# Gate loop and low-rank mixer on one core: a newly planned order of 2,210 operations

## The chip, the cores and the metric

The kernel runs on one core of a Trainium2 chip. Its time is the device time of that core in microseconds (us); three runs of the kernel before are given, and the profile describes one further execution. The engines are TensorE (PE in the profile, its weight loads PEld), VectorE (DVE), ScalarE (ACT), GpSimd (POOL) and SyncE (SP). Each works through its own queue in order.

## What is computed

Two blocks, one behind the other. The first is a recurrence over 768 steps with complex gates for 4 x 8 heads of width 48; the second mixes over the sequence through a matrix of rank 32 and then over channels:

```python
mag = np.sqrt(a_re * a_re + a_im * a_im)
scale = np.minimum(mag, 0.999) / (mag + 1e-06)      # a_re, a_im are multiplied by it
for t in range(S):                                   # S = 768
    S_re, S_im = ar*S_re - ai*S_im + k[t] v[t]^T,  ar*S_im + ai*S_re
    y[t] = q[t] @ S_re
x = y, as (batch 4, 768, 384)
h = x.transpose(0, 2, 1) @ U @ V                     # U 768 x 32, V 32 x 768
u = x + h.transpose(0, 2, 1)
out = u + np.maximum(u @ w_ch1, 0.0) @ w_ch2         # 384 -> 1536 -> 384
```

U, V, w_ch1 and w_ch2 arrive as 64-bit floats, which the kernel turns into 32-bit ones itself.

## The kernel before

**Tiling.** The sequence is cut into chunks of 128 steps: 6 for each batch element, 24 in all (`NCH`, `NT`). Two chunks make a group (`GC`, 12 groups).

- `gates(g)` works on a group: squares, logarithms and exponentials of the gates (`magnitudes`), sums along the chunk as products with a triangular matrix (PE tiles `es ps` and `ph`, lines 690 to 762), their exponentials `es`, angles `F` and waves `cs` (`turns`, `waves`). From group 3 on the operands are split into two parts first (`GS`, lines 677, 678, 750, 751). For each chunk but the first of a batch element POOL adds the last row of the angles before it to the new ones by a small DMA (line 742, `gate<-F`).
- `prep(i)` weighs q and k of a chunk by `es` and `cs` on DVE (`qk`, `QKC`), transposes them on PE in 64-row tiles (`tr`, line 817) and copies them out on ACT (`QK`).
- `chain(i)` does the chunk's own products (`inner`, `dk`, `y`: lines 846, 866, 895, 903), all in 64-row or 64-column tiles, and leaves the chunk's output in `xo`.
- `mixer(m)` works on two chunks: the rank-32 products (`rank`, `mixed`), transposed input `uTp`, the first channel matrix (`up`, line 992, or a scheme with fewer products, `few`, line 1104) and the second (`down`, lines 1193 and 1236). For the first two chunks the first channel product runs ahead of the rank-32 step and is then corrected by four small products (`up more`, line 1032, tiled by 32 rows); DVE adds each correction (line 1038) and so frees the PSUM bank for the next. There are two banks for `up` and `down` tiles, six for the rest.
- `single` and `weights` turn the weights (lines 583 to 589), and three differences of parts of w_ch2 are formed (line 617, `stage`, ops 88 to 90).
- `judge` (lines 1362 to 1379) checks that the fast way is valid: DVE collects extremes (`least`, line 712; `bad`, line 658), a product counts the violations (op 2208, `bad ps`), and DVE writes the count into `flag` (op 2209, line 1378; op 2207 makes its last operand). At the end every engine loads `flag` (line 1396) and branches on it (line 1406) around a general version of the kernel, which isn't run here.

**The order.** Nothing is issued when it is written down. `PE(...)`, `ACT(...)`, `DVE(...)`, `POOL(...)` and `SP(...)` each add an operation to a `Plan`, with a cost, a rank, what it reads and writes, and, for PE, `way`: a code of the tiling that its products use (0 the whole array, 1 64 columns, 3 64 x 64, 4 32 rows, 5 64 rows). Operations are numbered as they are added, 0 to 2209; "op 692" is such a number. `Plan.order` then issues them in the sequence of the constant `ORDER`, after asserting that each comes behind what it needs and that ring buffers are free. As every engine's queue is in order, `ORDER` fixes the five queues; across queues semaphores decide. An operation is several instructions (16 transpositions for a `tr`, 6 for a `down`, 8 for a `few`).

`SPARE` names operations of PE ahead of which idle products are issued: `idle(n)` (lines 1379 to 1388) multiplies the identity matrix into a PSUM tile that the following operation overwrites, two PE instructions each. Nobody reads them.

Some numbers that come up later: op 0 loads the triangular matrix `prefix_z`, op 3 is its copy on POOL, op 4 its scaling on ACT; op 95 is the first table load of ACT, ops 91 to 94 the loads of the first gates, op 96 their squares; op 199 is the first `tr`; ops 655 and 658 are the `es ps` products of group 4 (chunks 8 and 9), op 648 an ACT step ahead of them, op 683 the last wave that op 691 needs; op 691 is the DVE product that makes the first operand `QKC` of chunk 6, op 692 its transposition; ops 416, 419, 422 and 425 are the corrections, ops 417, 418, 420, 421, 423, 424, 426 and 427 DVE's adds behind them; ops 1750 and 1752 are the angle of one late chunk and the cast of the next chunk's angles, with op 1751, POOL's small transfer, between them.

Of the kernel before, what the change touches and what calls it, by code (L numbers as in the profile page):

```python
# [15 lines left out]
OP = mybir.AluOpType  # L16
# [99 lines left out]
)  # L116

SPARE = {
    125: 2, 135: 9, 184: 1, 199: 21, 203: 1, 223: 2, 250: 3, 412: 2,
}  # L120

DUMP = None
# [195 lines left out]
def kernel(  # L318
# [154 lines left out]
    w2 = singles.tile([128, KF, DM], FP, name="w2")  # L473
# [19 lines left out]
    def w2_of(x, y):  # L493

        return w2.rearrange("p (j x) m -> p j x m", x=2)[:, :, x, y * DH:(y + 1) * DH]
# [960 lines left out]
```

## Time and profile before

| | us |
|---|---|
| three runs | 559.97, 560.68, 565.65 |
| median | 560.68 |
| span of the profiled execution (first to last instruction) | 559.4 |
| first product of PE starts | 11.05 |
| last addition of DVE starts | 554.54 |
| busy in the span: PE, DVE, ACT, POOL | 533.3, 432.3, 317.7, 32.2 |

The profiled execution's own time is known as its span, 559.4 us; the time around it isn't shown apart. The fastest run lies 0.6 us above this span and the median 1.3.

How to read the lines: a group has the source line, engine, operation, output and inputs with their shapes and a count, then the busy time, the mean in ns of one, and the idle time ahead of it with what ended most of it. A wait has the engine and line that waited, whom it waited for, the total, how often and the longest. In the timeline and in the chain the first number is the start and the second the length. A row of the windows has the stretch, its length, and the busy time of PE, weight loads, DVE, ACT and POOL with the number of instructions, then the clock granted to TensorE (1.00 is full), the share of DMA time and GB/s. "q" behind an engine means its sequencer. For a transfer the last number is the median time from issue to landing.

### The profile page before, as it was taken

How to read it: one execution, taken by the hardware profiler on the slowest of the kernel's cores; microseconds unless marked ns; L12 is line 12 of the kernel's file. 1: busy time of each engine (PE TensorE's matmuls, PEld its weight loads, DVE VectorE, ACT ScalarE, POOL GpSimd, SP SyncE). 2: the span in 40 equal slices, each digit the busy share in tenths (PEclk: the TensorE clock that was granted, in tenths of full speed). 3: DMA queues.
4: the chain of work that ended last, by engine and by line, in shares of the span. 5: the costliest groups of instructions: out<-in, count | busy, mean ns of one | idle time of the engine just before them, and what ended most of it. 6: DMA issues, size and time to landing. Idle time of an engine off the chain costs nothing.

```text
span 559.4 us, 16683 instructions
## 1 busy us (share of the span) xinstructions
PE 533.3 (95%) x7242; PEld 481.8 (86%) x7242; DVE 432.3 (77%) x828; ACT 317.7 (57%) x553; POOL 32.2 (6%) x61
## 2 busy tenths in 40 slices
PE   2899999989999999999999999999999999999996
PEld 1677786867799997999999997899999989999996
DVE  6999989899799998898896976977572726728352
ACT  6889999894657869576567855861323322111110
POOL 1000000000011000101001001001000000000000
PEclk9999999989999999999999999999999999999999
DMA  9969876331333254133342235020011000000001
GB/s 222 198 145 201 195 182 184 91 52 37 85 66 80 45 107 76 37 69 65 60 91 51 57 52 110 16 40 27 9 36 36 4 2 22 8 8 22 21 9 33
DMA packets 150687, 39.90 MB, mean 71 GB/s; under 512 B 145912, under 2 KB 147408, under 8 KB 150608
## 3 DMA queue, kind: packets, MB, share of 16 engines
q1 hardware_dynamic: 148400, 34.43, 31.2%
q0 software_dynamic: 2208, 4.35, 2.3%
q8 instruction: 58, 0.95, 0.7%
q14 instruction: 21, 0.17, 0.1%
HBM read 33.60 MB, written 4.76 MB: 69 GB/s over the span
## 4 chain that ended last, share of the span: by engine, by line
PE 53%; DVE 20%; issue 7%; ACT 4%; DMA 3%; POOL 0%; SPq 0%; DVEq 0%; ACTq 0%; POOLq 0%
PE down L1236 20%; PE few L1104 17%; PE dk L866 3%; PE tr L817 3%; ACT gate L439 2%; DMA gate<-F 2%; PE inner L846 2%; DVE xo L445 2%; PE y L903 2%; DVE QKC L442 2%; PE up L992 1%; DVE qk L442 1%; PE y L895 1%; DVE GS L751 1%; DVE GL L671 1%
## 5 line engine op out<-in xcount | busy, mean ns | idle before, releaser
L1112 ACT COPY h<-few 128x512 f32<-128x512 f32 x60 | 34.8, 584 | 86.0 <-PE few L1104 84.6
L439 ACT ACTIVATE gate<-gate 128x768 f32<-128x768 f32 (+2 forms) x74 | 65.9, 901 | 16.6 <-DVE GS L751 9.0
L1236 PE MATMUL down<-w,h 128*128 128x192 f32 x396 | 72.7, 330 | 0.2 <-DVE xo L445 0.2
L1236 PEld LDWEIGHTS down<-w,h 128*128 128x128 f32 x396 | 64.5, 190 | 2.7 <-DVE xo L445 1.1
L445 DVE TENSOR_TENSOR xo<-down,xo 128x192 f32<-128x192 f32 (+1 forms) x79 | 29.8, 386 | 41.9 <-PE down L1236 39.7
L823 ACT COPY QK<-tr 112x512 f32<-112x512 f32 x96 | 50.0, 596 | 20.3 <-PE tr L817 20.1
L1104 PE MATMUL few<-extra,w 128*128 128x128 f32 x400 | 50.2, 276 | 0.1
L1104 PEld LDWEIGHTS few<-extra,w 128*128 128x128 f32 x400 | 47.6, 192 | 0.7 <-PE mixed L961 0.4
L1116 DVE CUSTOM_DVE_ANT_1 h<-few,h 128x512 f32<-128x512 f32 x60 | 40.2, 686 | 8.1 <-PE few L1104 4.3
L442 DVE TENSOR_TENSOR QKC<-qk,cs 128x768 f32<-128x768 f32 x48 | 44.5, 952 | 0.8 <-PE tr L817 0.6
L445 DVE TENSOR_TENSOR h<-few,h 128x512 f32<-128x512 f32 x30 | 20.5, 687 | 23.8 <-PE few L1104 12.6
L1236 PE MATMUL down<-stage 128*128 128x192 f32 x198 | 38.0, 329 | 0.5 <-DVE xo L445 0.5
L1180 POOL DMA_DIRECT2D out_dram<-xo x32 | 18.1, 573 | 276.8 <-DVE xo L445 248.5
L1236 PEld LDWEIGHTS down<-stage 128*128 128x128 f32 x198 | 32.6, 190 | 1.7 <-DVE xo L445 1.4
L992 PE MATMUL up<-uT,w 128*128 128x256 f32 x144 | 32.4, 382 | 0.2 <-ACT uT L981 0.2
L1104 PE MATMUL few<-gate,w 128*128 128x128 f32 x240 | 31.8, 277 | 0.1
L817 PEld LDWEIGHTS tr<-ident,QKC 64*112 64x112 f32 x768 | 25.2, 135 | 7.5 <-DVE QKC L442 2.5
L436 ACT ACT_TABLE_LOAD x24 | 30.8, 1283 | 1.1 <-PEq L1440 0.7
L817 PE MATMUL tr<-ident,QKC 64*112 64x64 f32 x768 | 29.8, 226 | 1.4 <-DVE QKC L442 1.4
L992 PEld LDWEIGHTS up<-uT,w 128*128 128x128 f32 x144 | 27.0, 190 | 4.4 <-ACT uT L981 0.6
L1104 PEld LDWEIGHTS few<-gate,w 128*128 128x128 f32 x240 | 29.1, 192 | 0.3 <-PE few L1104 0.2
L439 ACT ACTIVATE cs<-F 128x384 f32<-128x384 f32 x48 | 24.1, 520 | 8.1 <-DVE F L765 7.9
(161 smaller groups left out, 1106.2 us busy)
## 6 DMA issues: line engine op xcount, KB each, us to landing
stage<-in_moe_w_ch_dram SPq DMA_DIRECT2D x12, 768.0 KB, 5.4
gate<-in_a_im_dram SPq DMA_DIRECT2D x24, 192.0 KB, 3.0
gate<-in_a_re_dram SPq DMA_DIRECT2D x24, 192.0 KB, 3.7
qk<-in_q_dram SPq DMA_DIRECT2D x24, 192.0 KB, 4.4
qk<-in_k_dram SPq DMA_DIRECT2D x24, 192.0 KB, 3.6
VP<-in_v_dram SPq DMA_DIRECT2D x24, 192.0 KB, 3.9
out_dram<-xo POOLq DMA_DIRECT2D x12, 192.0 KB, 2.2
out_dram<-xo POOLq DMA_DIRECT2D x20, 96.0 KB, 1.9
```

The source lines that it names most:

```text
L436: ACT(1.37, rank, lambda: nc.scalar.preload_act_table_set(name), writes=[TABLE])
L439: return nc.scalar.activation(out=o, in_=i, func=f, **kw)
L442: nc.vector.tensor_tensor(out=o, in0=a, in1=b, op=OP.mult)
L445: nc.vector.tensor_tensor(out=o, in0=a, in1=b, op=OP.add)
L817: nc.tensor.transpose(out=get(*ps[r])[0:DQ, h], in_=get(*qkc)[at, h].rearrange("p u d -> p (u d)")[:, 0:DQ], identity=ident[at, at], tile_ ...
L823: nc.scalar.copy(out=get(*QK)[:, u].rearrange("p (h t) -> p h t", t=CH)[:, :, r * HC:(r + 1) * HC], in_=get(*ps[r])[0:DQ])
L992: nc.tensor.matmul(out=get(*ps)[:, e], lhsT=w1[:, f, (ff + e) * 128:(ff + e + 1) * 128], rhs=get(*uT)[:, f], start=(f == 0), stop=(f == KD ...
L1104: nc.tensor.matmul(out=get(*ps)[:, q], lhsT=w()[:, q * 128:(q + 1) * 128], rhs=v[0](), start=(n == 0 and q == 0), stop=True, skip_group_ch ...
L1112: ACT(c_act(n3 * CH) - 0.045, RU, lambda i=i, k=k: nc.scalar.copy(out=at(i, k), in_=get(*ps)), [ps], [o])
L1116: DVE(c_dve(n3 * CH), RU, lambda i=i, k=k: nc.vector._custom_dve(dve_ops.TENSOR_ADD_SAT, out=at(i, k), in0=get(*ps), in1=at(i, k), s0=math ...
L1180: queue.dma_start(out=out[b, c * CH:(c + 1) * CH, lo:hi], in_=get("xo", i)[:, lo:hi])
L1236: nc.tensor.matmul(out=get(*to)[:, part], lhsT=x(j), rhs=y[:, j], start=(first and j == 0), stop=(j == KH - 1), skip_group_check=not first)
```

## The change

`ORDER` is replaced whole: the same 2,210 operations, with the same numbers, in another sequence. `SPARE` is replaced: 36 idle products ahead of five operations in place of 41 ahead of eight. And one dependency is written down that was implicit in the old sequence: the product with the part of w_ch2 that DVE turns in place for the second pair of chunks (line 1306) now names that step, `("turned w2", 0)`. No operation is added or removed. The new order is said to be planned from traced durations, counting each change of TensorE's tiling.

The diff, cut to the lines of `ORDER` that matter here (95 lines in the file; each side's first, then around ops 655 to 692, then around op 1751, then the flag and the end):

```diff
 ORDER = (
-    95, 93, 91, 94, 0, 92, 150, 5, 11, 96, 99, 149, 100, 152, 97, 3, 151, 4, 98, 101, 194, 115, 112, 2, 116, 102, 195, 113, 106, 104, 196, 117, 114,
...
-    85, 652, 651, 653, 86, 655, 654, 465, 658, 656, 425, 87, 738, 657, 659, 661, 426, 660, 88, 662, 666, 739, 427, 89, 422, 682, 683, 685, 691, 686,
-    664, 667, 695, 692, 663, 668, 423, 701, 789, 715, 702, 693, 788, 669, 696, 694, 424, 703, 716, 740, 719, 416, 704, 814, 698, 90, 726, 813, 697,
...
-    1749, 1447, 1890, 1750, 1775, 1789, 1450, 1867, 1751, 1858, 1866, 1448, 1776, 1471, 1451, 1470, 1449, 1474, 1777, 1473, 1472, 1778, 1752, 1475,
...
-    1886, 1671, 1662, 1663, 1667, 1664, 1669, 1668, 1672, 1673, 1670, 1903, 1674, 1904, 2208, 1905, 1677, 2209, 1906, 1907, 1675, 1678, 1925, 1676,
...
-    2203,
+    0, 3, 4, 95, 91, 93, 92, 96, 99, 97, 98, 94, 101, 100, 102, 5, 103, 104, 115, 112, 106, 105, 113, 114, 7, 151, 107, 6, 117, 118, 120, 119, 121,
...
+    649, 456, 465, 83, 650, 651, 652, 460, 653, 84, 85, 132, 457, 616, 461, 654, 86, 655, 618, 656, 87, 658, 659, 657, 660, 81, 666, 458, 459, 661,
+    428, 738, 619, 681, 88, 683, 682, 425, 429, 504, 667, 426, 427, 691, 422, 505, 739, 692, 695, 668, 684, 430, 693, 696, 669, 694, 423, 685, 789,
...
+    1499, 1496, 1501, 1497, 1500, 1890, 1814, 1484, 1751, 1505, 1752, 1502, 1507, 1753, 1498, 1506, 1817, 1776, 1818, 1508, 1800, 1509, 1511, 1513,
...
+    2192, 2188, 2184, 2199, 2186, 2193, 2189, 2187, 2191, 2194, 2190, 2207, 2195, 2196, 2197, 2198, 2047, 2120, 2200, 2201, 2202, 2203, 2121, 2208,
+    2209, 2125,
 )
 
 SPARE = {
-    125: 2, 135: 9, 184: 1, 199: 21, 203: 1, 223: 2, 250: 3, 412: 2,
+    125: 3, 135: 5, 199: 23, 227: 4, 412: 1,
 }
...
-            product(one, 0, lambda j: of(0, 1)[:, j], w2_of(0, 1), names, first=False)
+            product(one, 0, lambda j: of(0, 1)[:, j], w2_of(0, 1), lambda half: names(half) + [("turned w2", 0)], first=False)
...
-                                                                    op=OP.subtract), [("w2s", 0)], ALL_W2)
+                                                                    op=OP.subtract), [("w2s", 0)], ALL_W2 + [("turned w2", 0)])
```

158 rows, old and new, of the table ORDER are left out of this document.

## The prediction

> **What bounds the kernel now.** First the page: busy times, then the slices.
>
> ```profile
> span 559.4 us, 16683 instructions
> PE 533.3 (95%) x7242; PEld 481.8 (86%) x7242; DVE 432.3 (77%) x828; ACT 317.7 (57%) x553; POOL 32.2 (6%) x61
> ...
> PE   2899999989999999999999999999999999999996
> ...
> DVE  6999989899799998898896976977572726728352
> ```
>
> TensorE (PE) is busy for 95% of the span, and the order leaves its 7242 products as they are. So a new order can only take from the other 26 us, from the changes of tiling, and from products that run slowly. In the first eight slices or so (to about 120 us) DVE is nearly always busy; after that PE alone is full. The second view is the waits, here of the first 131 us; its last row is from the waits after that.
>
> ```profile
> PE es ps L696 <- DVE GL L445: 11.1, 1, 11.1
> DVE GL L671 <- ACT GL L439: 3.6, 1, 3.6
> ...
> DVE GS L750 <- DMA gate<-F: 5.3, 5, 3.5
> ```
>
> PE starts at 11 us. DVE waits once 3.6 us for ACT, and later 3.5 us for one small transfer. The third view is the windows, the fourth the timeline around 120 us, where PE waits for DVE in a knot: at the corrections (L1032) and at the transpositions of chunk 6 (L817).
>
> ```profile
> 117.10:120.50 3.40, 1.51 (x8) 0.71 (x10) 3.40 (x6) 3.37 (x7) 0.00 (x0) 1.00 0.46 88
> 120.50:127.30 6.80, 6.60 (x120) 5.36 (x119) 6.80 (x9) 5.73 (x10) 0.77 (x1) 0.50 0.51 76
> ...
> 118.25 0.42 DVE L1038 CUSTOM_DVE_ANT_0 extra<-up,extra 128x256 f32<-128x256 f32 x1
> 118.58 1.35 DVE L617 TENSOR_TENSOR stage<-w 128x1152 f32<-128x1152 f32 x1
> 118.72 0.29 PEld L1032 LDWEIGHTS up<-V,more 32*128 32x128 f32 x2 [1.38 <-DVE extra L1038]
> ...
> 122.45 0.90 PEld L817 LDWEIGHTS tr<-ident,QKC 64*112 64x112 f32 x16 [0.92 <-DVE QKC L442]
> ```
>
> The columns after the window's length are busy PE, weight loads, DVE, ACT, POOL, then the granted clock. From 117.1 PE works 1.51 of 3.4 us; a DVE instruction of 1.35 us (L617) stands between two of those (L1038) that free its banks. In the 6.8 us after that the clock is 0.50.
>
> **The change, term by term.** The sum is made against the profiled execution, 559.4 us. That lies 1.3 under the median of the runs, 560.68, which I add at the end.
>
> *Changes of tiling.* On PE's queue, idle products included, the planner's tiling code changes 166 times in the old order and 153 times in the new (counted from ORDER). The price is read from the chain:
>
> ```profile
> 450.56 2.15 PE down L1236 x12
> ...
> 495.15 1.95 PE down L1236 x12
> ...
> 20.53 4.85 PE L1388 MATMUL tr<-ident 128*128 128x128 f32 x42
> ```
>
> Twelve "down" products that follow full-array products and precede others take 1.95 us; between tiled products (L866 before, L895 behind) they take 2.15. Two changes cost 0.20 us, one 0.10. Thirteen fewer: 13 x 0.10 = **-1.3** (0 if all of them lay in waits). The idle products go from 41 to 36. I cost them at nothing: they stand before products whose operands DVE has not made yet, as op 199. Without that cover five would be worth 5 x 0.23 = 1.2 us (the last row: 21 of them, two matmuls each, in 4.85 us).
>
> *The head.* The new order puts the ACT copy of prefix_z (op 4) and the transfer behind it (op 0) ahead of the first table load and the gate loads.
>
> ```profile
> 0.74 1.28 ACT L436 ACT_TABLE_LOAD   x1 [0.74 <-PEq L1440]
> ...
> 2.75 0.71 SPq L531 DMA_DIRECT2D prefix_z<-in_spans_dram  x1
> ...
> 4.97 0.84 ACT L439 ACTIVATE gate<-gate 128x768 f32<-128x768 f32 x1 [2.95 <-DMA gate<-in_a_re_dram]
> ...
> 6.18 0.65 POOL L535 CAST prefix_r<-prefix_z 128x128 fp32r<-128x128 f32 x1 [3.94 <-DMA prefix_z<-in_spans_dram]
> 6.87 0.31 ACT L439 ACTIVATE prefix_z<-prefix_z 128x128 f32<-128x128 f32 x1 [1.06 <-POOL prefix_r L535]
> ...
> 7.67 0.84 ACT L439 ACTIVATE gate<-gate 128x768 f32<-128x768 f32 x1
> ...
> 9.38 0.52 ACT L439 ACTIVATE GL<-GL 128x384 f32<-128x384 f32 x1
> ```
>
> The transfer took 3.4 us from issue to the cast. Issued at 0.7 it lands at about 4.1; cast 0.65, copy 0.31 and table load 1.28 put the squares at 6.3 at most, not 4.97: up to +1.4. Queued behind the waiting copy is every ACT instruction, and DVE and PE wait for them. Against it, the two ACT instructions of chunk 1 in the last rows (0.84 and 0.52) no longer stand between the steps of chunk 0's chain: -1.4. I take the head at **0**, between -1.4 and +1.4; from there to the first transposition DVE's queue is the bound. On SP the small TD writes move ahead of the loads of `qk` of chunk 1, so SP stands until ACT has made `es` of chunk 1, and these loads stand behind it. DVE needs them only after chunk 0's two operands are made; that covers them, and if it didn't, DVE's wait would be the price. On POOL output stores change places, which nobody waits for.
>
> *DVE ahead of chunk 6.* Of the 168 operations in DVE's queue ahead of op 691, the last one before chunk 6's first transposition (op 692), six move behind it and none comes in: one L617, one `mixed` add, one `uT` copy, three `least`.
>
> ```profile
> L617 DVE TENSOR_TENSOR stage<-w,stage 128x1152 f32<-128x1152 f32 x2 | 2.7, 1350 | 0.0
> L445 DVE TENSOR_TENSOR xo<-mixed,xo 128x384 f32<-128x384 f32 x24 | 12.3, 550 | 0.5 <-PE mixed L961 0.5
> L983 DVE COPY uT<-uTp 128x384 f32<-128x384 f32 x12 | 6.5, 552 | 0.4 <-PE uTp L977 0.2
> L712 DVE TENSOR_TENSOR least<-least,T 112x16 f32<-112x16 f32 x12 | 2.0, 168 | 0.1
> ```
>
> 1.35 + 0.55 + 0.55 + 3 x 0.17 = 2.96 us; an instruction starts 0.09 before the end of the one ahead (118.25 + 0.42 against 118.58), so 2.96 - 6 x 0.09 = 2.4. Of PE's own products ahead of op 692 one `uTp` operation moves behind it (three products like the idle ones, 3 x 0.115 = 0.3) and has to be made up later; the rest are the same. PE's waits so shrink by 2.4 - 0.3: **-2.1**. Ends: -3.0, and 0 if ACT, not DVE, sets op 691.
>
> *The half clock.* Op 692 no longer waits right behind the corrections, and no L617 stands between ops 426, 427 and 423, 424, so I expect no stretch like 117.1 to 120.5 and no half clock. Its price, from the chain:
>
> ```profile
> 125.44 1.89 PE tr L817 x32
> ...
> 443.96 1.04 PE tr L817 x32
> ```
>
> The same 32 transpositions take 1.89 us in it and 1.04 at full clock. Of the 4.85 us from 122.45 to 127.30 that is 4.85 x (1 - 1.04 / 1.89) = 2.2 lost; some products there are not set by the clock. **-2.0** (0 to -2.2). [...] The windows show the fall right behind a stretch that was thin, not idle, so I go by them.
>
> *The late knot.*
>
> ```profile
> 341.85 0.55 DVE L765 SCALAR_TENSOR_TENSOR F<-F,ph 128x384 f32<-128x384 f32 x1 [1.12 <-ACT F L439]
> ...
> 347.40 0.36 DVE L750 CAST GS<-gate 128x384 fp32r<-128x384 f32 x1 [3.48 <-DMA gate<-F]
> ...
> 350.29 0.92 PE L961 MATMUL mixed<-r,V 64*128 64x192 f32 x8 [1.60 <-DVE G L442]
> ```
>
> Between F (op 1750, ready at 342.40) and the cast that needs the transfer from it (op 1752) DVE has two operations, and the transfer takes until 347.40; DVE stands, and `mixed` waits 1.60. In the new order eleven DVE operations stand between the two. **-1.6** (0 if another of the fifteen such transfers takes its place).
>
> *The end.* Ops 2207 to 2209 form the flag that chooses the general path. In the old order it is there at 438; in the new one its product (op 2208) is PE's last and its cast (op 2209) DVE's last. Every engine loads the flag and branches on it before it can finish.
>
> ```profile
> L1378 DVE CAST flag<-bad ps x1: 138/138/138, 438.1 to 438.1; 1x1 int32<-1x1 f32 x1
> ...
> 542.51 0.54 POOL L1180 DMA_DIRECT2D out_dram<-xo  x1 [15.08 <-DVE xo L445]
> ...
> out_dram<-xo POOLq DMA_DIRECT2D x20, 96.0 KB, 1.9
> ...
> L1396 POOLq TENSOR_LOAD <-flag x1: 493/493/493, 542.5 to 542.5; - x1
> ...
> L1406 PEldq COMPARE_BRANCH x2: 90/1912/3735, 552.0 to 554.7; - x2
> ...
> L1451 POOLq EVENT_SEMAPHORE x4: 17/17/17, 558.6 to 559.3; - x4
> L1451 POOLq DRAIN x3: 46/112/3974, 548.3 to 559.1; - x3
> ...
> 554.54 0.36 DVE L445 TENSOR_TENSOR xo<-down,xo 128x192 f32<-128x192 f32 x1 [0.42 <-PE down L1236]
> ```
>
> POOL needs 9.8 us from its load of the flag (542.5) to the end of its drain (548.3 + 4.0); some 1.1 of it it waits for its last store (issued at 542.5, landed 1.9 later, while its load and branch of the flag take 0.8), which will be long done; so 8.7. Today that is hidden behind PE. In the new order the flag is ready behind the last add, at about 555.0 on the old time; POOL then drains until 563.7, and its closing semaphores (558.6 to the end, 0.8) put the end at 564.5: **+5.1**. Ends: if the drain takes 0.11, its median, the end is 560.6, +1.2; PE's own branch of 3.7 us gives +1.0; if the landing still counts, +6.2.
>
> Sum: 559.4 - 1.3 - 2.1 - 2.0 - 1.6 + 5.1 = 557.5; with 1.3 for the median, **558.8**.
>
> **The rivals.** *A short end.* POOL's other two drains take 0.05 and 0.11 us, so the long one may be a wait for something that is over by then; against it, it starts at 548.3 with its stores landed. Time: 558.8 - 3.9 = 554.9.
> *The front gives nothing, and it ends slower.* ACT is nearly as full as DVE up to 120 us, and its queue ahead of the wave that op 691 needs (op 683) is only three operations shorter. If the copy of prefix_z costs ACT its 1.4 us at the head, op 692 starts no earlier: 558.8 + 2.1 + 2.0 = 562.9. It decides if chunk 6's first transposition starts at 122 us or later. For it: the 3.6 us for which DVE waited for ACT. Against it: that very ACT step (op 648) has five operations less in front.
> *A new thin stretch.* The new order has less PE work ahead of the `es` products of group 4 (op 655: an `up`, a `mixed` and two `uTp` operations fewer), so PE can now wait there for DVE. If a window gets thin, the clock halves for another 6.8 us: up to half of it lost, 3.4, on top of the front's loss 562.9 + 3.4 = 566.3.
> *The tiling count does nothing*, since the drains lie in waits: 558.8 + 1.3 = 560.1.
>
> **How the numbers follow.** Forecast as summed, with the tiling count or without: 0.50. Short end 0.27; front lost 0.13; thin stretch 0.10. The likeliest case has its own range of 556 to 561. With every end at its best (-1.4, -1.3, -3.0, -2.2, -1.6, +1.0) it is 552.2, at its worst (+1.4, 0, 0, 0, 0, +6.2) 568.3. For 8 in 10 I take 553 to 565: the short end and the lost front are in it, the thin stretch and the corners are not. One per cent, about what a measurement of this kernel can tell from no change, is 5.6 us: faster means under 555.1, slower over 566.3. Faster: most of the short end (0.20) and a corner of the forecast (0.06), 0.26. Slower: half of the thin stretch and a late wait not seen (0.12). Within: 0.62.
>
> **What would show it.** Changes: twelve "down" products in a row keep 1.95 and 2.15. Chunk 6: its first transposition at about 120, not 122.45, and a granted clock of 1.00 from 113 to 131. Late knot: the wait of L750 for `gate<-F` under 2 us in sum. End: the last add at about 547.5 (554.5 less 7.0), the `flag` cast behind it, then POOL's load, branch and a drain of 4 us, and some 10 us between the last add's start and the end, not 4.9. The prediction is wrong if the drain is short, if PE's waits in the first 131 us are not smaller, or if a new wait of over 2 us stands on PE behind 131.

## The result, and the profile after

The changed kernel takes 566.0 us (median of 8 runs, 564.57 to 567.45); the kernel before took 561.6 beside it. The ratio is 1.0076, with a 95% interval of 1.0052 to 1.0101: slower by three quarters of a per cent. The forecast was 558.8, with a range of 553 to 565. Two single runs stand far off, one of the kernel before here (2982.67 us) and one of more_changes below (1068.71); the ratios leave them out. The profiled execution of the changed kernel took 566.48 us, with a span of 564.7 (559.4 before).

The page of the changed kernel, its first lines and PE's row of the slices:

```profile
span 564.7 us, 16665 instructions
PE 529.3 (94%) x7232; PEld 479.7 (85%) x7232; DVE 435.8 (77%) x828; ACT 321.9 (57%) x554; POOL 32.3 (6%) x61
...
PE   2889999999999999999999999999999999999992
```

PE is busy for 4.0 us less (533.3 before), since ten idle matmuls and thirteen changes of tiling are gone and, as shown below, 3.4 us less pass at half clock; and yet the span is 5.3 us longer. The last slice of PE reads 2 where it read 6: something stands behind PE's last product. The views of three source lines at the end, and the timeline there:

```profile
L1396 POOLq TENSOR_LOAD <-flag x1: 493/493/493, 554.9 to 554.9; - x1
...
L1406 POOLq COMPARE_BRANCH  x2: 38/39/40, 555.5 to 557.2; - x2
...
L1451 POOLq EVENT_SEMAPHORE  x4: 17/17/17, 563.9 to 564.6; - x4
...
L1451 POOLq DRAIN  x3: 46/112/3973, 559.9 to 564.4; - x3
```

```profile
554.49 0.36 DVE L445 TENSOR_TENSOR xo<-down,xo 128x192 f32<-128x192 f32 x1 [1.39 <-PE down L1236]
554.76 0.14 DVE L1378 CAST flag<-bad ps 1x1 int32<-1x1 f32 x1
```

The flag is there at 554.90, POOL loads it at once, branches until 557.2, and its drain of 3.97 us starts at 559.9 and ends at 563.9; the closing semaphores take the rest. From the start of the last add to the end are 10.2 us, where there were 4.9. So the end went as forecast (+5.3 for +5.1). But the last add starts at 554.49, where it started at 554.54; the forecast was 547.5. **Of what the front and the late knot were to give, nothing is left at the end.**

Where it went shows best as a lag. For each operation I added up the usual duration of PE's real products ahead of it (for each kind of operation, the lower quartile in both traces of the time from its start to the next one's, and 0.10 more at a change of tiling; the idle ones left out), and took that from its start in the trace. What is left is time in which PE stood, ran slowly or did idle products. The difference of the lags, after less before:

| at | before: start, work ahead, lag | after | difference of the lags |
|---|---|---|---|
| first product | 11.05, 0, 11.05 | 9.92, 0, 9.92 | -1.1 |
| op 692, chunk 6's first transposition | 122.45, 87.9, 34.5 | 121.51, 88.0, 33.5 | -1.0 |
| op 431, first of the `down` products | 131.07, 94.4, 36.6 | 130.57, 95.6, 35.0 | -1.7 |
| op 1968, the last `rank` | 456.89, 413.8, 43.1 | 458.99, 414.5, 44.5 | +1.4 |
| op 2201, the last `down` | 553.37, 509.5, 43.9 | 553.31, 508.2, 45.1 | +1.2 |

The forecast was -2.1 at op 692, -4.1 at op 431 and -5.7 at the end. Instead the front gave 1.7 of its 4.1, and behind op 431 the lag grew by 2.9, where it was to shrink by 1.6. With the 1.3 us less of work and the 5.3 us more at the end that is -1.3 - 1.7 + 2.9 + 5.3 = +5.2, against +5.3 for the two spans.

The windows ahead of 131 us and behind it (busy PE, weight loads, DVE, ACT, POOL), first before, then after:

```profile
0.00:131.00 131.00, 112.36 (x1720) 88.47 (x1720) 117.86 (x202) 114.59 (x193) 4.02 (x16) 0.97 0.76 161
131.00:556.00 425.00, 420.90 (x5528) 393.31 (x5523) 314.46 (x626) 203.11 (x361) 28.20 (x45) 1.00 0.22 44
```

```profile
0.00:131.00 131.00, 111.59 (x1626) 87.12 (x1627) 118.44 (x198) 115.67 (x191) 4.04 (x16) 0.99 0.73 156
131.00:556.00 425.00, 417.70 (x5608) 392.59 (x5606) 317.41 (x631) 206.24 (x364) 28.23 (x45) 1.00 0.23 46
```

In the first 131 us PE stood for 18.6 us before and 19.4 after, so its waits there are not smaller, which the prediction had named as a sign of being wrong; what the front gave is in the clock (0.97 in this stretch before, 0.99 after) and in idle matmuls that are gone. Behind 131 us PE stood for 4.1 of 425 us before and 7.3 after; 1.5 and 1.4 of that lie behind its last product, so that 2.6 became 5.9. The view of PE's waits there, from 131 to 556, before and after:

```profile
PE mixed L961 <- DVE G L442: 1.6, 1, 1.6
PE down L1236 <- DVE xo L445: 0.7, 3, 0.3
```

```profile
PE down L1236 <- DVE xo L445: 1.6, 2, 1.1
PE few L1104 <- DVE gate L1076: 1.3, 1, 1.3
PE y L903 <- ACT xo L914: 1.0, 1, 1.0
PE dk L866 <- issue: 0.6, 2, 0.4
PE tr L817 <- ACT xo L914: 0.6, 1, 0.6
PE down L1236 <- DVE h L1228: 0.3, 1, 0.3
```

The stop at `mixed`, the old late knot, is gone as forecast. Eight others stand in its place, at 158, 204, 264, 296, 339, 377, 401 and 417 us, for several reasons as it will turn out. The experiments take the parts one by one.

### The profile page after: what moved, and what is told of

Read it like the earlier page. It is cut to its first block, busy times and chain, and to the rows that moved or that the text cites. A ratio compares the mean times of both kernels' runs of the same rounds, so it can differ in the third digit from the quotient of the medians.

```text
span 564.7 us, 16665 instructions
## 1 busy us (share of the span) xinstructions
PE 529.3 (94%) x7232; PEld 479.7 (85%) x7232; DVE 435.8 (77%) x828; ACT 321.9 (57%) x554; POOL 32.3 (6%) x61
## 4 chain that ended last, share of the span: by engine, by line
PE 71%; DVE 11%; ACT 8%; DMA 4%; issue 3%; SPq 1%; DVEq 0%; ACTq 0%
PE down L1236 25%; PE few L1104 23%; PE dk L866 3%; PE tr L817 3%; PE inner L846 3%; PE down L1193 3%; PE y L903 3%; ACT gate L439 2%; DMA gate<-F 2%; PE y L895 2%; DMA gate<-in_a_im_dram 2%; PE uTp L977 1%; PE mixed L961 1%; ACT cs L439 1%; PE rank L938 1%
## 5 line engine op out<-in xcount | busy, mean ns | idle before, releaser
L1112 ACT COPY h<-few 128x512 f32<-128x512 f32 x60 | 34.6, 585 | 89.6 <-PE few L1104 81.9
L439 ACT ACTIVATE es<-es ps 128x384 f32<-128x384 f32 x48 | 20.8, 495 | 23.2 <-PE es ps L692 20.3
L742 POOL DMA_DIRECT2D gate<-F x15 | 12.5, 832 | 328.5 <-DVE F L765 192.7
L866 PEld LDWEIGHTS dk<-VP,QKC 64*64 64x64 f32 (+1 forms) x1408 | 25.5, 130 | 6.7 <-issue 3.9
L866 PE MATMUL dk<-VP,QKC 64*64 64x48 f32 (+1 forms) x1408 | 28.6, 220 | 2.2 <-issue 2.0
```

What stands on the lines that cost most here:

```text
L439: return nc.scalar.activation(out=o, in_=i, func=f, **kw)
L866: nc.tensor.matmul(out=get(*dk[r])[x:end, h], lhsT=get(*ks)[at, h, x // DP, 0:end - x], rhs=get(*VPi)[at, h], start=True, stop=True, tile_ ...
L1112: ACT(c_act(n3 * CH) - 0.045, RU, lambda i=i, k=k: nc.scalar.copy(out=at(i, k), in_=get(*ps)), [ps], [o])
```

## The experiments

All times are medians. The kernels were run in four groups, each with runs of the kernel before beside it (561.85, 560.89, 561.49 and 561.32 us); the ratios are to those. The changed kernel was run only beside the 561.6 above, so a difference from its 566.0 is good to about 1 us. Edits are given as moves in an engine's queue; the rest of the order stays. In four of the kernels (early_flag, late_flag and the two with spread queues) the order takes more lines of text, so that their line numbers are 36 higher in the rows.

### The end: the flag early, and the flag late

```diff
 changed kernel, ORDER (early_flag)
-    ... 2191, 2194, 2190, 2207, 2195 ... 2203, 2121, 2208, 2209, 2125
+    ... 2206, 2207 ... 1694, 2208, 2209 ... 2191, 2194, 2190, 2195 ... 2203, 2121, 2125
 kernel before, ORDER (late_flag)
-    ... 2206, 1637, 1565, 2207 ... 1674, 1904, 2208, 1905, 1677, 2209 ... 2194 ... 2201, 2197, 2198, 2202
+    ... 2206, 1637, 1565 ... 1674, 1904, 1905, 1677 ... 2194, 2207 ... 2201, 2208, 2197, 2198, 2202, 2209
```

> The changed kernel, with ops 2207 to 2209 (the last operand of the flag, its product, its cast) moved ahead: op 2207 behind op 2206, the product and the cast behind op 1694, at about 462 us. Theory: the end is 5.3 us longer because POOL's load, branch and 3.97 us drain stand behind the late flag. Then the last add to the end takes 4.9 us again (10.2 in the changed kernel), POOL's load of the flag starts at about 542, and the time is 566.0 - 5.3 = 560.7. Rival: the drain waits for the last output transfers, which SP issues at 554.9, whatever the flag does: last add to end stays at 10.2 and the time at 566.0.

> The kernel before, with op 2207 behind op 2194, op 2208 behind PE's last product and op 2209 behind DVE's last add. Theory: last add to end goes from 4.9 to 10.2 us and the time from 561.6 to 566.9. Rival (the end doesn't hang on the flag): 4.9 and 561.6.

Measured: 559.87 us for early_flag (ratio to the kernel before 0.9976, 0.9949 to 1.0003), 6.1 less than the changed kernel, and 567.89 for late_flag (1.0107, 1.0063 to 1.0152), 6.0 more than the kernel before. In early_flag POOL loads the flag at 541.3 and its drain starts at 547.1, while PE works; the last add starts at 553.58 and the end is 5.2 us behind it:

```profile
L1432 POOLq TENSOR_LOAD <-flag x1: 493/493/493, 541.3 to 541.3; - x1
...
L1487 POOLq DRAIN  x3: 46/112/3973, 547.1 to 558.5; - x3
```

The same three small operations cost 6 us by the medians in either kernel when they stand last; when they stand early, POOL's load and drain lie behind PE's work. In the two traces of the changed order the end itself gives 5.0 of that, and the last add starts 0.9 sooner. early_flag has no half clock near 120 us (its mean granted clock is 0.998 over its runs, 0.992 in the changed kernel's), which is part of the difference. The long drain takes 3.97 us in the traces of both.

### The front: DVE's neighbours

DVE's queue up to and with op 691 (163 operations in the changed kernel, 169 before; ops 430, 620, 177, 343, 502 and 89 moved behind) is indeed shorter, by 2.8 us of work, and the waits of over 0.2 us in it fell from 7.8 to 4.4. Yet op 691 ends only 1.1 us sooner (121.26 against 122.40), from a start 0.7 later. The missing part lies between the instructions. The timeline of DVE in the changed kernel:

```profile
112.09 0.56 DVE L677 CAST GS<-GL 128x768 fp32r<-128x768 f32 x1
112.75 0.96 DVE L678 TENSOR_TENSOR GS<-GL,GS 128x768 fp32r<-128x768 f32 x1
113.63 0.55 DVE L587 TENSOR_SCALAR w<-w 128x768 uint32<-128x768 uint32 x1
114.10 0.17 DVE L712 TENSOR_TENSOR least<-least,T 112x16 f32<-112x16 f32 x1
```

L678 reads what the cast ahead of it wrote: it starts 0.10 behind the cast's end (112.09 + 0.56 = 112.65). L587 reads nothing of L678's: it starts 0.08 before L678 ends. Over the queue a free neighbour starts 0.08 before the end, a dependent one 0.03 behind it (20 pairs by the names of their tiles) or 0.10 (11 pairs); for all of them I count 0.043. The kernel before has 9 dependent neighbours ahead of op 691; the new plan puts a consumer right behind its producer 42 times. That is 33 x 0.126 = 4.2 us, more than all that the shorter queue gave. Less work and waits, -2.8 and -3.4, with +4.2 and the start 0.7 later make -1.3, close to the 1.1. The experiment moves 19 operations by one to three places (in the second kernel 60 over the whole queue), so that something else stands between.

```diff
 DVE's queue (spread_front; the first four of 19 moves)
-    108, 8, 9 | 12, 14, 124 | 116, 157, 156, 197, 198
+    8, 108, 9 | 12, 124, 14 | 116, 156, 197, 157, 198
```

> The changed kernel, with 19 DVE operations of the queue ahead of op 691 each moved by one to three places, so that 22 instead of 42 of them stand right behind an operation of DVE whose result they read (9 in the kernel before). Theory: such a neighbour costs 0.126 us, since a free instruction starts 0.083 us before the end of the one ahead and a dependent one 0.043 behind it; 20 x 0.126 = 2.5 us, chunk 6's first transposition starts at 119.0 to 119.5 instead of 121.5, and the time is 563.5 to 564. Rival: ACT sets the corrections and chunk 6; the transposition stays at 121.5 and the time at 566.0. Third case: the transposition comes at 119 and later waits on PE give it back, 566.0.

> The same for the whole of DVE's queue: 65 instead of 130 such neighbours (60 in the kernel before). Behind 131 us PE is the bound, so beyond the 2.5 us of the front only the late waits on DVE can shrink (1.3 us at 264, 1.1 at 419, 0.6 at 377): 561.5 to 564 by the theory, 566.0 by the rival that DVE's neighbours cost nothing that PE waits for.

Measured: 564.75 us (1.0054, 1.0024 to 1.0084) and 562.61 (1.0016, 0.9989 to 1.0043), which is 1.2 and 3.4 less than the changed kernel. The timeline of spread_front at the same place:

```profile
111.02 0.55 DVE L481 TENSOR_TENSOR xo<-mixed,xo 128x384 f32<-128x384 f32 x1
111.48 0.55 DVE L713 CAST GS<-GL 128x768 fp32r<-128x768 f32 x1
```

An add of `mixed` now stands between the cast and the operation whose result it reads (L671 in the changed kernel's numbering, which ends at 111.10). The cast starts 0.09 before that add ends (111.02 + 0.55 = 111.57); in the changed kernel it stood right behind its producer and started 0.11 behind its end (111.98). With 22 such neighbours the gaps shrink by 2.4 us, as expected. But op 691 ends at 120.64, only 0.6 sooner, because DVE's waits grew from 4.4 to 6.3 us: at 49 us for ACT (0.65 became 1.09), at 93 for PE's `rT` (0.67 became 1.35), at 103 for the `gate<-F` transfer (1.21 became 1.66). So both were true: the neighbours' price is real in DVE's queue, and behind it ACT, PE and a transfer set the front, much as the rival in the prediction had it. What the 0.6 is worth in time isn't settled: 1.2 us is about what such a difference is good to, and the trace of spread_front has no half clock near 120 us. The kernel with the whole queue spread gains 2.1 more beside the same runs of the kernel before; its edit differs behind 131 us, where DVE's adds come sooner to the banks that PE waits for.

### The head: a 25th table load

The timeline of ACT at the head of the changed kernel, then of the experiment, in which op 95 stands ahead of op 4:

```profile
2.69 1.28 ACT L439 ACT_TABLE_LOAD   x1 [2.69 <-DMA prefix_z<-in_spans_dram]
...
4.32 1.28 ACT L436 ACT_TABLE_LOAD   x1
5.69 0.84 ACT L439 ACTIVATE gate<-gate 128x768 f32<-128x768 f32 x1
```

```profile
0.74 1.28 ACT L436 ACT_TABLE_LOAD   x1 [0.74 <-PEq L1440]
...
5.45 0.84 ACT L439 ACTIVATE gate<-gate 128x768 f32<-128x768 f32 x1 [2.10 <-DMA gate<-in_a_im_dram]
```

```diff
 ACT's queue (table_first)
-    4, 95, 96, 101
+    95, 4, 96, 101
```

> The changed kernel with ACT's explicit table load (op 95) ahead of the copy of prefix_z (op 4). Theory: in the changed kernel the copy brings a 25th table load of 1.28 us, which stands at 2.7 us behind the transfer of prefix_z, and delays the squares of chunk 0 to 5.69 (4.97 before). Then there are 24 table loads, the squares start at about 5.0, PE's first product at 9.2 instead of 9.9, chunk 6 some 0.5 to 0.7 us sooner, and the time is 565.4. Rival: the gate loads set the head (DVE waits 3.1 us for one); the first product stays at 9.9, 566.0.

Measured: 565.2 us (1.008, 1.0055 to 1.0105), 0.8 less than the changed kernel, which is within the spread: the two ratios, 1.008 and 1.0076, are the same. With the copy in front, the program gets a table load of its own, which waits for the transfer of prefix_z, and the planned load follows: 2.56 us in place of 1.28. In the experiment it is one again. But the squares start at 5.45, not at 5.0: they then wait for `gate<-in_a_im`, and PE's first product comes at 9.67 (9.92 in the changed kernel). Op 692 starts at 120.35, 1.2 sooner than in the changed kernel and 1.0 or more sooner than in four other traces with the same front (121.4 to 121.9); that is one trace. Theory and rival each hold for a part, and what the load costs in time isn't settled.

### The half clock

```diff
 kernel before (before_warm)
-    DVE's queue: 426, 88, 427, 89          idle products: none ahead of op 692
+    DVE's queue: 426, 427, 88, 89          idle products: 6 ahead of op 692
```

> The kernel before with two edits at the thin stretch of 117 to 122 us: DVE's op 427 is put ahead of op 88 (L617), so that the second half of the corrections starts some 1.3 us sooner, and six idle products stand ahead of op 692 to fill PE's wait there. Theory: the half clock comes from the thin stretch. Then the profile shows no half clock near 120 to 127, the mean granted clock rises from about 0.991 to 0.994 or more, and the time falls by 2 to 3 us to about 559.5 (one us at half clock costs PE half a us; in the changed kernel's own runs those with a mean clock of 0.993 or 0.994 took 565.2, those with 0.988 to 0.992 took 566.9). Rival: the clock falls for another reason; it stays at 0.991 and the time at 561.8, or the waits gone alone give 0.5.

Measured: 560.04 us, 0.9974 (0.9951 to 0.9997), 0.85 less than the kernel before. The mean granted clock is 0.998 over its 12 runs, against 0.992 over the 22 beside it: some 6 us less at half clock. The theory's clock came about, but its 2 to 3 us did not, although the second half of the corrections (op 427) starts about 1 us sooner. That 0.85 isn't the price of the half clock, since the edit also delays op 692: it starts at 122.87, and at 122.95 in old_r_first, which has the same edit, against 122.45 before. The price is better read from op 692 to op 431, between which each order has the same products. In the old order PE takes 8.62 us from the one to the other in the kernel before and 8.49 in late_flag, each with 6.8 us at half clock, and 7.00 in old_r_first, with none: 1.6 us. In the new order it takes 7.8 us in the seven traces that have no half clock there, and 9.0 to 9.1 in the three with 3.4 us of it (the changed kernel, late_four, new_mended): 1.2 to 1.3 us. So the prediction's 2.0 for 6.8 us was somewhat high, but of the right kind.

The clock also bears on small differences between kernels. Of the changed kernel's eight runs the four with a mean clock of 0.993 or 0.994 took 565.3 in the median, the other four 566.8. Among runs at 0.993 to 0.995 alone, spread_front takes 564.5, spread_all 562.5, table_first 565.1, and no_false and late_four (below) 566.3 and 561.5. Against 565.3 the whole spread queue and late_four keep most of their gains; spread_front's shrinks to 0.8 and table_first's to 0.2.

The windows from 117.1 us, of the changed kernel and of before_warm:

```profile
117.10:120.50 3.40, 2.92 (x20) 1.85 (x19) 3.37 (x6) 3.36 (x6) 0.00 (x0) 1.00 0.68 106
120.50:123.90 3.40, 3.40 (x62) 2.90 (x64) 3.40 (x6) 2.89 (x7) 0.77 (x1) 0.64 0.19 35
123.90:127.30 3.40, 3.40 (x95) 2.90 (x88) 2.18 (x3) 2.19 (x5) 0.00 (x0) 0.86 1.00 187
```

```profile
117.10:120.50 3.40, 2.42 (x15) 1.51 (x14) 3.40 (x5) 3.37 (x8) 0.00 (x0) 1.00 0.39 77
120.50:123.90 3.40, 3.40 (x29) 3.04 (x29) 3.37 (x4) 3.10 (x6) 0.00 (x0) 0.53 0.48 46
```

In the profiled execution of the changed kernel the half clock is still there, for 3.4 instead of 6.8 us, behind a window in which PE was busy for 2.92 of 3.4 us; the profiled one of before_warm has it too, though by their mean clocks (0.998 or more in eight of the twelve, 0.996 in this one) most of its runs have not. PE's busy share of a window doesn't decide it alone: in the same trace of the changed kernel the 3.4 us from 261.4, with 2.08 busy, are followed by full clock. What makes it fall stays open.

### Late stops: written order, and a queue

The timeline of the changed kernel at the stop of 417 us:

```profile
414.19 0.36 DVE L445 TENSOR_TENSOR xo<-down,xo 128x192 f32<-128x192 f32 x1 [1.15 <-PE down L1236]
...
416.92 1.14 PE L1236 MATMUL down<-w,h 128*128 128x192 f32 x6
417.12 0.36 DVE L445 TENSOR_TENSOR xo<-down,xo 128x192 f32<-128x192 f32 x1 [2.02 <-PE down L1236]
...
419.17 1.24 PE L1236 MATMUL down<-w,stage 128*128 128x192 f32 x6 [1.11 <-DVE xo L445]
```

The second add (op 1613) takes the second half of a PSUM tile whose products were done when the first add started, at 414.2. It stands idle for 2.02 us and starts just behind op 1622, a product that fills the *first* half of the same tile anew and is written ahead of it in the new ORDER. The planner keeps parts of a tile apart (its operations name them); the waits of the program don't. Similarly, product 732 writes one part of its `y` tile and waits for copy 734, which reads another part. The first experiment leaves every engine's queue as it is and changes only which of two engines' operations is written first, at six places.

```diff
 ORDER (no_false; each engine's queue unchanged)
+    1075 ahead of 1083; 1153 ahead of 1161; 1613 ahead of 1621; 2184 ahead of 2192; 1535 ahead of 1543
+    732 ahead of 734
```

> The changed kernel with the same queue on every engine; only the order in which the program writes operations of different engines is changed at six places: five adds on DVE (ops 1075, 1153, 1613, 2184, 1535) are written ahead of, not behind, the products that fill the other half of the same PSUM tile (ops 1083, 1161, 1621, 2192, 1543), and the product 732 is written ahead of the copy 734. Theory: in the changed kernel these stand still without need, since each waits for the end of the neighbour's access to its own tile (the add 1613: products done at 414.2, started at 417.1, just behind op 1622). Then PE's stops at 158 (1.26 us), 377 (0.6) and 417 (1.27) go and the time is 566.0 - 3.1 = 562.9. Rival: they wait for their own data or for the engine's queue; the stops stay and the time is 566.0.

Measured: 566.28 us (1.0097, 1.0061 to 1.0133): nothing gained. The stops at 158 and 417 are gone, so the mechanism is right:

```profile
415.02 0.35 DVE L445 TENSOR_TENSOR xo<-down,xo 128x192 f32<-128x192 f32 x1
415.42 2.22 PE L1236 MATMUL down<-stage 128*128 128x192 f32 x12 [0.29 <-DVE xo L445]
```

Op 1613 now runs at 415.02, and PE waits 0.29 instead of 1.11. But at the places where the add really was late, the wait turned round: the product, now written behind the add, waits for it, at 327 (1.0 us), 377 (1.4) and 548 (0.7). The second experiment keeps the two moves that helped, and mends the other places in the queues.

```diff
 changed kernel (late_four)
+    ORDER: 1613 ahead of 1621; 732 ahead of 734; 1535 ahead of 1543
-    DVE's queue: 1266, 1309, 1032, 1310, 1038, 1024      1534, 1542, 1562, 1535
+    DVE's queue: 1266, 1032, 1024, 1309, 1310, 1038      1534, 1535, 1542, 1562
-    ACT's queue: 1785, 1861, 1784, 1786, 1863, 1811, 1810, 1809
+    ACT's queue: 1785, 1784, 1786, 1811, 1810, 1809, 1861, 1863
```

> The changed kernel with five stops of PE behind 131 us taken out where each arises: product 732 written ahead of the copy 734 (stop at 158, 1.26 us); DVE's ops 1032 and 1024 put ahead of the cast 1309, which waits for a gate<-F transfer (stop at 264, 1.3); DVE's add 1535 put right behind 1534 and written ahead of product 1543 (377, 0.5); ACT's two cs operations 1861 and 1863 put behind the copy 1809 (401, 0.8); the add 1613 written ahead of product 1621 (417, 1.27). Theory: the late part lost what the front and the old knot gave because of these stops, and they are independent; the time is 566.0 - 4.9 = 561.1. Rival: a stop taken out comes back at the next place, as it did when adds were moved for their program order alone (566.28 in place of 562.9); then 565 to 566.

Measured: 562.04 us (0.9992, 0.9964 to 1.002), 4.0 less of the 4.9 expected. PE's waits from 131 to 556:

```profile
PE dk L866 <- issue: 1.6, 2, 1.1
PE tr L817 <- DVE QKC L442: 0.6, 1, 0.6
PE down L1236 <- DVE xo L445: 0.3, 1, 0.3
```

The five stops went; 0.6 came back at 165 us, and the waits called "issue" grew.

### Late stops: PE's own instructions

What "issue" is, the fourth kernel shows. PE stops at 76.2 us inside a row of short products and resumes at 77.52, while nothing that the product reads is late. In the profiles of early_flag, spread_all and table_first, which have the same products in the same order up to there, it stops behind the same matmul, the 983rd with the idle ones counted; in those of no_false and spread_front, where the transfers had ended earlier (75.0 and 74.3), it passes that one without a stop. In the instruction queue a transfer of 16 KB ran from 74.6 to 76.1. Such stops of the traces before, after and of fetch_phase resume 1.4 to 1.7 us behind the end of such a transfer.

```diff
 SPARE, changed kernel (fetch_phase)
-    125: 3, 135: 5, 199: 23, 227: 4, 412: 1
+    125: 3, 135: 5, 199: 15, 227: 4, 412: 1
```

> The changed kernel with 15 instead of 23 idle products ahead of op 199, nothing else, so that 32 instructions (16 products and 16 weight loads) fewer stand ahead of everything behind 25 us. Theory: PE's four stops inside long rows of short products (77 us, behind product 29 of 32 of op 374; 204, behind 11 of 16 of op 928; 339, behind 25 of 32 of op 1778; 456, behind 16 of 32 of op 1962) are waits for PE's own instructions, which come in 16 KB pieces; each resumes 1.3 to 1.6 us behind the end of such a transfer. Then they keep their place in the count of instructions and fall 16 products later: in op 375 behind its 13th, at the end of op 1962, and those of 204 and 339 into long products (down, rank), where they vanish. Time 566.0 - 1 = 565. Rival: they wait for data or a bank; they stay at the same product of the same operation, 566.0.

Measured: 566.86 us (1.0108, 1.0057 to 1.0159). The timeline of the changed kernel, then of the experiment:

```profile
75.39 0.79 PE L866 MATMUL dk<-VP,QKC 64*64 64x48 f32 x29
...
77.52 0.69 PE L866 MATMUL dk<-VP,QKC 64*64 64x48 f32 x35 [1.35 <-issue]
```

```profile
75.21 1.23 PE L866 MATMUL dk<-VP,QKC 64*64 64x48 f32 x45
...
77.16 0.47 PE L866 MATMUL dk<-VP,QKC 64*64 64x48 f32 x19 [0.72 <-issue]
```

The stop moved from behind the 29th of these 64 products to behind the 45th, sixteen later, just the matmuls of the eight idle products that were left out (32 instructions with their loads, 16665 to 16633); the stops at 204 and 339 vanished, and the one at 456 moved to the end of its operation, all as expected of waits for instructions. The time did not fall: a new stop of 1.5 us came at 87 us, again 1.65 us behind the end of such a transfer, the clock was 0.50 for the 3.4 us from 89.6, and op 692 starts at 124.29, 2.8 later than in the changed kernel. An estimate from the page of the changed kernel, which counts 59 transfers in that queue (`q8 instruction: 59, 0.97`) and 7232 matmuls with as many weight loads: if all 59 are PE's, one holds about 245 of these instructions. The short products come every 0.027 us (1.23 us for 45), each with its weight load, so that some 122 of them would use up a transfer in 3.3 us. The new order has four such stops (1.57, 0.59, 0.48 and 0.34 us, 3.0 in sum, counted from one start to the next) where the kernel before has one that is clear (1.0, inside `inner` at 32 us); whether it is longer rows of short products that make the difference wasn't tested. That the eight idle products had cost nothing isn't shown by this run, as its new stop and its clock hide it.

### The old late knot

The old knot was put down to DVE, which waits 3.48 us for a transfer. Two kernels test that.

```diff
 kernel before with the edits of before_warm
 old_mended (also seven of DVE's dependent neighbours spread)
-    DVE's queue: 1752, 1753, 1892, 1780, 1781
+    DVE's queue: 1780, 1892, 1781, 1752, 1753
 old_r_first
-    ACT's queue: 1779, 1817, 1476, 1794
+    ACT's queue: 1779, 1476, 1817, 1794
```

> The kernel before with the mends that apply to it: op 427 ahead of op 88 and six idle products ahead of op 692 (measured 0.85 alone), the cast 1752 and op 1753 put behind op 1781 so that the wait for gate<-F holds nobody up (the stop of 1.6 us at 350), and seven of DVE's dependent neighbours spread. Theory: 561.2 - 0.85 - 1.6 = 558.7 or a little less, so that the mended new order is 6 to 7 us ahead of the mended old one. Rival: the new order brings nothing of its own, and both mended kernels are within 2 us of each other.

> The kernel before with op 427 ahead of op 88 and six idle products ahead of op 692 (alone 560.04), and on ACT the copy r<-rank (op 1476) put ahead of op 1817. Theory: the stop of 1.6 us at 350 was not DVE's wait as such; ACT's op 1817 waits 2.3 us for the sum behind the transferred gate, takes 1.48 us, and the copy that the product mixed needs stands behind it (putting DVE's cast later left the stop at 2.0 us). Then the stop goes and the time is 560.0 - 1.6 = 558.4. Rival: the copy of op 1817, 0.46 us later, holds up DVE's op 1818 and the stop comes back behind it; 560.0.

Measured: 561.59 us (1.0002, 0.9971 to 1.0032) and 560.06 (0.997, 0.9948 to 0.9992). Both theories failed. In old_mended `mixed` still waits, for 2.0 us:

```profile
348.22 1.48 ACT L439 ACTIVATE gate<-gate 128x1536 f32<-128x1536 f32 x1 [2.82 <-DVE GS L751]
349.61 0.46 ACT L944 COPY r<-rank 128x384 f32<-128x384 f32 x1
...
350.12 0.92 PE L961 MATMUL mixed<-r,V 64*128 64x192 f32 x8 [2.02 <-ACT r L944]
```

ACT waits for the sum behind the transferred gate, computes 1.48 us, and only then copies what `mixed` reads; in the kernel before the same stands behind the wait that the profile had put down to DVE. With the copy in front (old_r_first) `mixed` starts 0.82 sooner (348.74 against 349.56 in before_warm), and its stop shrinks to 0.2 us, but PE loses 0.6 inside `rank` (2.82 us for 2.25 in before_warm), where the profile shows no releaser, and `y` waits 0.31 and 0.18 for ACT's copies: some 1.2 us in sum, against 1.3 in before_warm. What holds PE up is ACT again for the copies, and stays open for `rank`. So the knot looks like ACT's backlog more than any single wait, which these two runs suggest and don't prove.

### Does the number of changes count?

```diff
 PE's queue, changed kernel, behind 131 us (more_changes; two of 14 swaps)
-    dk, dk, down, down        down, down, yin, yin
+    dk, down, dk, down        down, yin, down, yin
```

> The changed kernel with 14 neighbouring pairs of products behind 131 us swapped so that the tiling changes 181 instead of 153 times; nothing else moves. Theory: a change costs 0.10 us wherever PE is the bound; 28 x 0.10 = 2.8, time 568.8, less what the swaps take from the waits for instructions. Rival: changes lie in waits and cost nothing; 566.0.

Measured: 568.83 us (1.0124, 1.0086 to 1.0161); without the run far off it is 568.5, so 2.5 to 2.8 more than the changed kernel, as 28 x 0.09 to 0.10 has it. The change's own term holds where PE is the bound.

### Everything that helped

```diff
 changed kernel (new_mended): the edits of early_flag, table_first, late_four, and DVE's whole queue spread (62 moves)
```

> The changed kernel with all mends at once: the flag early (measured 6.1 alone), DVE's dependent neighbours spread over its whole queue (3.4), the table load ahead of the copy (0.8), and the five late stops taken out (4.9 by the theory). If they add up: 550.8; as the spread queue already shortened the late stops by some 1.3, 552. Rival: they overlap further and give half of the last two: 555.

Measured: 552.95 us (0.9822, 0.978 to 0.9864), 13 less than the changed kernel and 8.5 less than the kernel before. Its page, and PE's waits from 131 to 556:

```profile
span 552.5 us, 16664 instructions
```

```profile
PE dk L866 <- issue: 1.2, 2, 0.6
PE down L1236 <- DVE xo L445: 0.3, 1, 0.3
PE y L895 <- issue: 0.2, 1, 0.2
```

6.1 + 3.4 + 0.8 + 4.0 is 14.3, so the mends add up but for 1.3 us, about as well as such differences are known. What is left behind 131 us are mostly the waits called "issue" (1.4 of 1.7). The last add starts at 547.53, which is where the forecast had it (547.5), though by other means. Against the best kernel with the old order (before_warm, 560.04) it is 7.1 ahead. How much of that belongs to the new order isn't shown: the old order was given fewer mends, and those of old_mended and old_r_first gained nothing on before_warm.

## Why the prediction was wrong

Against the span of the profiled execution the steps were to give 557.5, and the span is 564.7. In order of the terms:

- *Changes of tiling*, -1.3: right. PE's work ahead of its last product is 1.3 us less by the table of lags: eleven changes between real products, and the flag's product moved to the end. The 28 added changes of more_changes gave 0.09 to 0.10 each.
- *The head*, 0: PE's first product came 1.1 sooner, in spite of a table load that the diff doesn't show: the copy put ahead of the first planned table load brought one of its own (1.28 us, at 2.69), and DVE's queue started 0.7 later. Neither was in the sum. The squares started at 5.69, where 6.3 at most was costed.
- *DVE ahead of chunk 6*, -2.1: **the step that failed first.** Op 692 came 0.9 sooner and its lag fell by 1.0, half of the forecast, and no more than the first product had brought. The six operations and their 2.4 us are right. What failed is "an instruction starts 0.09 before the end of the one ahead": I took that pitch for all, from a queue that held 9 dependent neighbours, and used it for one that holds 42, where such a neighbour costs 0.126 us more. When the gaps were taken out again (2.4 us in spread_front), op 691 came only 0.6 sooner, as ACT, PE and a transfer stood right behind. So the rival that ACT sets the front carried more than its 0.13, though not the whole front was lost.
- *The half clock*, -2.0: the price was about right (6.8 us of it cost 1.6 in the old order), but I took it to go altogether, and 3.4 us of it stayed in the profiled execution, which cost 1.2 to 1.3. That a thin stretch brings it isn't shown: it fell behind 2.92 busy us of 3.4, and elsewhere not behind 2.08. From op 692 to op 431 the lag fell by 0.7.
- *The late knot*, -1.6: **the step that failed most.** The wait is gone, but the low end, "0 if another of the fifteen such transfers takes its place", left no room for new stops. One such transfer did take its place (264 us, 1.3); two more stops came from the written order of parts of one tile, one from ACT's queue, one from an add behind other adds, and the stops called "issue" came to 0.6, where the view of before had none. In sum the lag grew by 2.9 behind op 431 instead of falling by 1.6, and the mends of five stops brought 4.0 back. The two waits by written order are in none of the dependencies by which the order was planned.
- *The end*, +5.1: right, +5.3 in the two traces (10.2 for 4.9), 6.0 and 6.1 by the medians of the two experiments.

The range ended at 565.0. Its upper end held the front lost, which came to half, but counted behind 131 us only what might not be gained, not what a new order can lose there; the corner of 568.3, left out as unlikely, took the late knot at 0, where it was +2.9.

## What to carry to other kernels

A plan made from durations must also count what lies between instructions: here a consumer right behind its producer (0.126 us each on DVE), a second table load (1.28 us), waits that the program makes for a whole tile where the plan knows its parts (1.0 and 1.1 us of waiting on PE at 158 and 417 us), and stops inside rows of short products, which behave like waits for instructions (four, 3.0 us). When an order is planned anew, compare how often each of these occurs in the old and the new order before pricing the gain, and expect losses where the old order was already full. And what every engine needs before it can finish belongs early: three small operations, put last, cost 5 to 6 us.

## What the runs showed of the hardware

- POOL's closing drain takes 3.97 us in each of five traces (before, after, early_flag, late_flag, new_mended) and starts 2.5 to 2.7 us behind its branch on the flag (545.8 and 548.3 before, 557.2 and 559.9 after); from the load of the flag to the end of that drain are 9.0 us after (554.9 to 563.9).
- Inside rows of short products PE stood for 0.3 to 1.5 us at a time, while nothing that the product reads was late, and resumed 1.4 to 1.7 us behind the end of a 16 KB transfer in the instruction queue, at a place that moved with the count of instructions (16 matmuls later for 16 matmuls and 16 loads less). That is what a wait for instructions would do.
- The granted clock fell to half behind a window with PE busy for 2.92 of 3.4 us, and not behind another with 2.08 in the same trace; 3.4 us of it cost 1.2 to 1.3 between the same two operations of the new order, and 6.8 us 1.6 in the old.
- DVE started an independent instruction 0.08 us before the one ahead had ended, and a dependent one 0.03 us behind it (20 pairs ahead of op 691 in the changed kernel) or 0.10 (11, with the pair at 112 us).
